# A retention layer and a gated feed-forward on one core: the last 256 tokens of batch 1 in 64-token chunks, with the casts of their states on VectorE, and three state groups of batch 0 as 64x64 tiles

## The chip, the cores and the metric

The kernel runs on one core of a Trainium2 chip. The metric is the device time of one execution in microseconds; the median of three runs of the kernel before is 297.26 us (297.23 to 297.26). A profiled execution of each kernel shows where the time goes: TensorE (PE; PEld are its weight loads), VectorE (DVE), ScalarE (ACT), GpSimd (POOL), and SyncE (SP), which issues nearly all transfers.

## The reference

Eight batches of eight heads, 576 tokens, head size 64. Retention is attention without a softmax: the scores are multiplied by a power of a per-head decay. The result, laid out by token, goes through a feed-forward of width 2048.

```
gamma = 1.0 - 2.0 ** (-5.0 - np.arange(H))
rel = pos[:, None] - pos[None, :]
Dmat = np.where(rel >= 0, gamma[:, None, None] ** rel, 0.0)
attn = np.matmul(scores * Dmat, v)                  # scores = q k^T / 8
x = attn.transpose(0, 2, 1, 3).reshape(B * S, H * D)  # 4608 x 512
h = x @ w_in                                        # 512 x 2048
out = (h / (1 + exp(-beta * h))) @ w_out            # 2048 x 512
```

## The kernel before

Because the decay is a power of the distance, it is split into a factor on q and one on v (`gq`, `gv`), and retention can be done in chunks: inside a chunk the masked scores times v, and from earlier chunks q times a running state, the sum over earlier tokens of k^T v. A state is 64x64 for each head. All matmuls are in bf16 and sum in PSUM, which has eight banks; the tags `mm` (three banks), `O` (two), `sc` (two) and `st` (one) are handed round, and a tile that is written into a bank waits for the reader of the tile before it.

The first 512 tokens of each batch are a block of the feed-forward; the last 64 tokens of all eight batches make a ninth block ("tail"). The feed-forward of a block is a list of fills: `up` (one 128-wide slice of w_in: four matmuls of 512 columns into `mm`, then a ScalarE activation into `gT`; or half a block of tokens, with 256 columns) and `down` (four of the 16 products for 128 tokens; the last four end in a copy and an output transfer). The retention of the next block is put between the fills. `merged` does this by hand-written positions: each step of a stream has a number, and is emitted ahead of the fill of that number. `u1` is the first fill of block 1, `d0` the first `down` of block 0, `base[n]` the first fill of block n. The engines execute in the order of emission, each in its own queue.

Retention is done in three ways.

- Batch 0 works on spans of 256 tokens (`s_T`, `s_sc`, `s_O`, `s_st`, `s_keep`, `s_cross`, `s_x`), at the start of the kernel, when nothing else can fill TensorE. `s_st(a, n, s, rows)` adds k^T v of head group a (four heads) over some rows of a span; with `low` or `high` rows it uses 64 of the 128 rows of the array and all 128 columns. `s_keep` copies the 64x64 blocks on the diagonal into `sbds`, which `s_cross` reads as a 128x128 block-diagonal weight.
- Batch 1 works on chunks of 128 tokens, i = 4 to 7 (`t_k` turns the keys, `a_sc` scores, `a_O` products, `a_cross` states times q, `a_st` states, `a_x` evicts the result). Chunks 4 and 5 come under the last `down` fills of block 0; chunks 6 and 7 under the first `up` fills of block 1. Those first `up` fills go over the first 256 tokens (ten slices in halves) while the last 256 are not there yet.
- Batches 2 to 7 and the tail work on chunks of 64 tokens, with 64x64 tiles in all four quarters of the array (`d_st` states, with a `chain` of sums on VectorE and casts on ScalarE; `d_sc` scores; `d_out` products and crosses). `spread` and `head_of` order the heads so that four matmuls that follow each other use four different quarters. For these, q and k are stored with heads 4 to 7 swapped in pairs (`turned`), from batch `QB` on. In `d_out` a VectorE memset, the fence, separates two sets of matmuls that add to the same PSUM places from different rows of the array.

The keys are cast and the values scaled on GpSimd (`pre`), q of batches 0 and 1 is scaled on VectorE (`pre_q`), and the order of transfers on SyncE is q and kv of batch 1, then of batch 2, and so on.

Of the kernel before, what the change touches and what calls it, by code (L numbers as in the profile page):

```python
# [19 lines left out]
def kernel(  # L20
# [15 lines left out]
    P = 128  # L36
# [33 lines left out]
    QB = 2  # L70
# [211 lines left out]
    def pre_q(b, n):  # L282
# [15 lines left out]
        e.tensor_tensor(batch[b]["qs"][:, cs, hs], q_tiles[b][:, hs, cs].rearrange("p h i d -> p i h d"),  # L298
                        gq[:, cs, hs].unsqueeze(3).to_broadcast([P, cs.stop - cs.start, hs.stop - hs.start, D]),
                        ALU.mult)  # L300
# [97 lines left out]
    def a_cross(i):  # L398

        b, c = seq[i]  # L400
        if c == 0:
            return
        for p in range(HP):
            rhs, view = q_cols(i, slice(0, P), p)
            nc.tensor.matmul(view(O_of(i, p)), sbds[c - 1][:, p, :], rhs, start=False, stop=True, skip_group_check=True)

    def a_O(i):
# [5 lines left out]
        for j, p in [(n % 2, n // 2) for n in range(H)]:  # L413
            nc.tensor.matmul(O_of(i, p)[j * D:(j + 1) * D], vn[:, 2 * p + j, :], R[:, j, p, :],
                             start=opens(i, p), stop=c == 0, skip_group_check=True)
# [11 lines left out]
    def a_st(i):  # L427

        b, c = seq[i]
        if b is None:  # L430
            return
        L = live[i]
        if c == 0:
            state_ps[b] = psum.tile([P, HP, P], F32, name="st", tag="st", bufs=1)
        st = state_ps[b]
        for p in range(HP):
            nc.tensor.matmul(st[:, p, :], heads(L["kn"], p), heads(L["vn"], p),
                             start=(c == 0 and p == 0), stop=True, skip_group_check=True)
        for j in range(2):
            r, cols = slice(j * D, (j + 1) * D), slice(j * D, (j + 1) * D)  # L440
            e = nc.vector.tensor_copy if i in (CB + 2, CB + 3) else nc.scalar.copy
            if c < CB - 1:
                e(sbds[c][r, :, cols], st[r, :, cols])
                continue
            e(ends[b][r, :2], st[r, :2, cols])
            e(ends[b][(1 - j) * D:(2 - j) * D, 2:], st[r, 2:, cols])
# [72 lines left out]
    def s_st(a, n, s, rows, at=None, fresh=False):  # L519
# [4 lines left out]
        S, at = spans[s], 2 * a if at is None else at  # L524
        for i in range(2):
# [31 lines left out]
    def d_sc(u):  # L557

        R = [sb.tile([P, 2, 2, HP, TL], BF16, name="R", tag="R", bufs=4) for _ in range(2)]
        sc = {}  # L560
        for x in range(2):
# [384 lines left out]
```

## Time and profile before

| what | value |
|---|---|
| median of three runs | 297.26 us |
| the profiled execution | 297.28 us |
| its span, first to last instruction | 295.5 us |
| granted TensorE clock | 1.00 throughout |
| VectorE, ScalarE, GpSimd busy | 35%, 49%, 38% |
| transfers, share of 16 engines | over 0.9 for most of the first 220 us |
| all transfers | 53.97 MB in 124033 packets |

The page shows busy time by engine, the span in 40 slices, the chain of work that ended last, and groups of instructions by source line. A matmul's length in the trace runs on past the start of the next one, since matmuls are pipelined; how long one takes in a stream is read from start to start. The field "128*128" of a matmul row is the part of the array, rows by columns, that it uses; "128x512" is what it streams.

Where the changed steps stand, from the timeline (start to start): batch 0's half-row states lie at 12.96, 13.85 and 19.86 us; the retention of batch 1 between 42.1 and 55.4 us; the first `down` of block 1 at 66.2 us; batch 2's retention from 67.2 us on. In the stretch from 43.8 to 55.4 us TensorE is busy all of the time, VectorE 8.0, ScalarE 8.6 and GpSimd 9.2 of its 11.6 us.

### The profile page before, as it was taken

What the parts mean: (1) busy time and instruction counts of PE and PEld (TensorE: products, weight loads), DVE (VectorE), ACT (ScalarE), POOL (GpSimd) and SP (SyncE); (2) the same over time, 40 slices, a digit from 0 to 9 for tenths busy, and PEclk for the clock granted to TensorE, in tenths of its full rate; (3) what the DMA queues carried; (4) which work ended last, traced back from release to release, by engine and by line L of the source; (5) the groups of instructions that cost most, each with busy time, mean ns of one, the idle gap of its engine ahead of it and who ended that gap; (6) DMA issues with size and microseconds to landing.
All of it is one profiled execution on the core that took longest, in us unless ns stands there. A gap on an engine that the chain in (4) does not pass through costs nothing.

```text
span 295.5 us, 7656 instructions
## 1 busy us (share of the span) xinstructions
PE 287.1 (97%) x3245; PEld 150.6 (51%) x3274; DVE 102.5 (35%) x213; ACT 145.9 (49%) x255; POOL 111.1 (38%) x219
## 2 busy tenths in 40 slices
PE   7999999999999999999999999999999999999995
PEld 3654587855544554445444544454554544444443
DVE  5764546604640551045204530354053500110012
ACT  5657537783278434843474347434780167007600
POOL 5957027955733713280438316754223000000000
PEclk9999999999999999999999999999999999999999
DMA  7999999999999898949999849998998110131011
GB/s 225 306 367 386 376 226 277 220 180 253 222 229 235 214 162 231 252 72 161 231 250 198 180 105 273 190 177 180 219 174 138 73 38 0 35 71 38 0 71 71
DMA packets 124033, 53.97 MB, mean 183 GB/s; under 512 B 101840, under 2 KB 116448, under 8 KB 124000
## 3 DMA queue, kind: packets, MB, share of 16 engines
q1 hardware_dynamic: 123968, 53.49, 82.1%
q8 instruction: 25, 0.41, 0.6%
q14 instruction: 8, 0.07, 0.1%
q10 hardware_dynamic: 32, 0.01, 0.0%
HBM read 36.71 MB, written 9.44 MB: 156 GB/s over the span
## 4 chain that ended last, share of the span: by engine, by line
PE 96%; DMA 1%; issue 1%; ACT 0%; DVE 0%; DVEq 0%
PE po L690 42%; PE ph L655 38%; PE ph L670 4%; PE O L614 2%; PE sc L568 1%; PE st L586 1%; DMA qn<-in_q_dram 1%; PE O L627 1%; PE T L352 1%; PE st L527 1%; PE sc L378 0%; PE sc L490 0%; PE O L504 0%; ACT kT L475 0%; PE ph L248 0%
## 5 line engine op out<-in xcount | busy, mean ns | idle before, releaser
L690 PE MATMUL po<-w_out_sb,gT 128*128 128x512 bf16 (+3 forms) x619 | 125.7, 358 | 2.3 <-issue 2.1
L657 ACT ACTIVATE gT<-ph,beta_sb 128x512 bf16<-128x512 f32 (+1 forms) x140 | 91.5, 659 | 50.9 <-PE ph L655 50.5
L655 PE MATMUL ph<-xT,w_in_sb 128*128 128x512 bf16 (+1 forms) x550 | 114.4, 364 | 0.5
L690 PEld LDWEIGHTS <-gT 128*128 128x128 bf16 x636 | 60.2, 98 | 60.7
L655 PEld LDWEIGHTS <-w_in_sb 128*128 128x128 bf16 x560 | 54.3, 98 | 57.5 <-DVE first L594 0.4
L697 DVE COPY ot<-po 128x512 f32<-128x512 f32 (+2 forms) x33 | 22.2, 672 | 72.2 <-PE po L690 69.4
L328 POOL CAST kn<-kvn 128x128 bf16<-128x128 f32 (+2 forms) x76 | 23.4, 343 | 46.1 <-DMA kvn<-in_k_dram 41.2
L295 POOL TENSOR_TENSOR qs<-qn,gq 128x256 bf16<-128x256 f32 (+1 forms) x36 | 26.3, 756 | 33.1 <-DMA qn<-in_q_dram 33.1
L575 DVE TENSOR_TENSOR R<-sc,tri 128x512 bf16<-128x512 f32 x28 | 17.4, 684 | 60.0 <-PE sc L568 60.0
L306 POOL TENSOR_TENSOR vn<-kvn,gv 128x512 bf16<-128x512 f32 x28 | 29.1, 1040 | 7.4 <-DMA kvn<-in_v_dram 7.1
L642 ACT CAST xT<-O 128x512 bf16<-128x512 f32 x14 | 7.5, 590 | 31.6 <-PE O L627 31.6
L597 ACT CAST sbd<-warm 128x256 bf16<-128x256 f32 x18 | 7.3, 407 | 25.6 <-DVE warm L594 20.6
L670 PE MATMUL ph<-xT,w_in_sb 128*128 128x512 bf16 x54 | 12.8, 379 | 0.1
L594 DVE TENSOR_TENSOR first<-st,warm 128x256 f32<-128x256 f32 x24 | 10.2, 425 | 2.9 <-ACT sbq L597 0.5
L316 POOL TENSOR_TENSOR kn<-tln,gq 128x128 bf16<-128x128 f32 (+1 forms) x12 | 5.6, 470 | 14.2 <-DMA tln<-in_q_dram 9.9
L594 DVE TENSOR_TENSOR warm<-st,first 128x256 f32<-128x256 f32 x18 | 7.6, 423 | 9.6 <-PE st L586 8.4
L673 ACT ACTIVATE gT<-ph,beta_sb 128x512 bf16<-128x512 f32 x14 | 8.7, 688 | 4.4 <-PE ph L670 4.4
L642 DVE CAST xT<-O 128x512 bf16<-128x512 f32 x14 | 9.0, 686 | 5.1 <-PE O L627 5.1
L214 POOL CAST w_in_sb<-wt 128x256 bf16<-128x256 f32 (+1 forms) x15 | 7.7, 530 | 5.0 <-DMA wt<-in_moe_w_in_dram 4.9
L597 ACT CAST sbd<-first 128x256 bf16<-128x256 f32 x18 | 7.3, 407 | 2.2 <-DVE first L594 0.2
L670 PEld LDWEIGHTS <-w_in_sb 128*128 128x128 bf16 x56 | 5.2, 97 | 6.3 <-issue 0.5
L231 DVE TENSOR_SCALAR w_out_sb<-wt,rbeta_sb 128x512 bf16<-128x512 f32 x13 | 5.9, 485 | 5.0 <-DMA wt<-in_moe_w_out_dram 5.0
(107 smaller groups left out, 166.1 us busy)
## 6 DMA issues: line engine op xcount, KB each, us to landing
qn<-in_q_dram SPq DMA_DIRECT2D x16, 512.0 KB, 5.2
kvn<-in_k_dram SPq DMA_DIRECT2D x32, 256.0 KB, 6.1
kvn<-in_v_dram SPq DMA_DIRECT2D x32, 256.0 KB, 5.1
out_dram<-ot SPq DMA_DIRECT2D x31, 256.0 KB, 3.4
wt<-in_moe_w_out_dram SPq DMA_DIRECT2D x8, 512.0 KB, 8.5
wt<-in_moe_w_in_dram SPq DMA_DIRECT2D x5, 512.0 KB, 8.8
wt<-in_moe_w_in_dram SPq DMA_DIRECT2D x6, 256.0 KB, 5.6
tln<-in_q_dram SPq DMA_DIRECT2D x8, 128.0 KB, 3.6
```

The source lines that it names most:

```text
L295: nc.gpsimd.tensor_tensor(batch[b]["qs"][:, cs, to], q_tiles[b][:, hs, cs].rearrange("p h i d -> p i h d"), gq[:, cs, hs].unsqueeze(3).to_ ...
L306: nc.gpsimd.tensor_tensor(live[i]["vn"], kv_tiles.pop(i)[:, 1], gains(gv, c), ALU.mult)
L328: nc.gpsimd.tensor_copy(kn[:, c % 2, to], t[:, 0, hs])
L575: nc.vector.tensor_tensor(R[x][:, j].rearrange("k c p q -> k (c p) q"), sc[x, j].rearrange("k c p q -> k (c p) q"), mask, ALU.mult)
L594: nc.vector.tensor_tensor(new[:], add, sums[(c - 1) % 2][:], ALU.add)
L597: nc.scalar.copy((sbq[c] if c < NC - 1 else ends[u])[:], new[:])
L642: (nc.scalar.copy if n % 2 else nc.vector.tensor_copy)(x, o)
L655: nc.tensor.matmul(ph, w_in_sb[:, ko, fo * P:(fo + 1) * P], xts[m][:, ko, :, w], start=(ko == 0), stop=(ko == KO - 1))
L657: nc.scalar.activation(gts[m][:, fo, :, w], ph, ACT.Silu, scale=beta_sb[:, fo:fo + 1])
L670: nc.tensor.matmul(phs[f][:], w_in_sb[:, ko, f * P:(f + 1) * P], xts[m][:, ko], start=(ko == 0), stop=(ko == KO - 1))
L690: nc.tensor.matmul(po[:, x:y], gT[:, fo, ms, :], w_out_sb[:, fo, n0 + x:n0 + y], start=(fo == 0), stop=(fo == FO - 1), skip_group_check=m ...
L697: (nc.scalar.copy if m == 0 else nc.vector.tensor_copy)(ot, po[:, :nn])
```

## The change

Batch 1's chunks 6 and 7 (256 tokens) leave the 128-token way. They become four chunks of 64 tokens, by `late_scores` (at u1 + 3: `d_st(1, 1)`, then `d_sc` of the second half alone, then the `chain`, with its casts on VectorE, then the two masks) and a new `half_out` (at u1 + 12), which is `d_out` for half a batch. The first 256 tokens stay in two chunks of 128, but states are now kept as 64x64 tiles in `sbq` and as fp32 sums in `sums`, so that the chain can go on from them: `a_st` uses 128x64 tiles, `a_cross` 64x64 tiles, and `a_keep` copies. For that batch 1 takes the swapped order of heads (QB = 1): heads 4 to 7 of its q are scaled in two steps each, and its keys are cast in three steps each on GpSimd. `t_k(7)` moves ahead of the first `up` fill of block 1.

The number of `up` slices of block 1 in halves goes from 10 to 15 (NH). Products of `down` that are split into two of 256 columns: block 0 from slice 8 on (before: from 5), block 1 from slice 12 on (before: none). In batch 0, `s_st` of heads 0 to 3 over half the rows uses 64x64 tiles, two for each pair of heads, and the first such group comes ahead of the whole-span group.

```diff
-    QB = 2
+    QB = 1
...
         if b < 2:
             hs, cs = slice(n // 2 * HP, (n // 2 + 1) * HP), slice(n % 2 * 2, n % 2 * 2 + 2)
-            e = nc.vector
+            for to, hs in [(hs, hs)] if n < 2 or b < QB else turned[1:]:
+                nc.vector.tensor_tensor(batch[b]["qs"][:, cs, to], ..., ALU.mult)
...
     def a_cross(i):
         b, c = seq[i]
-        if c == 0:
-            return
         for p in range(HP):
-            rhs, view = q_cols(i, slice(0, P), p)
-            nc.tensor.matmul(view(O_of(i, p)), sbds[c - 1][:, p, :], rhs, start=False, stop=True, skip_group_check=True)
+            for j in range(2):
+                rhs, view = q_cols(i, half(j), p)
+                nc.tensor.matmul(view(O_of(i, p)[half(head_of(b, p, j) % 2)]), sbq[2 * c - 1][half(j), p, :], rhs,
+                                 start=False, stop=True, skip_group_check=True)
...
     def a_st(i):
...
+        for p in range(HP):
+            for j in range(2):
+                nc.tensor.matmul(state_ps[b][half(j), p, :], L["kn"][:, 2 * p + j, :], L["vn"][:, head_of(b, p, j), :],
+                                 start=c == 0 and p == 0, stop=True, skip_group_check=True)
+
+    def a_keep(i):
+        b, c = seq[i]
+        nc.scalar.copy(sbq[2 * c + 1][:], state_ps[b][:])
+        if c:
+            nc.vector.tensor_copy(sums[c % 2][:], state_ps[b][:])
...
     def s_st(a, n, s, rows, at=None, fresh=False):
...
+        if a == 0 and rows != whole_span:
+            for i in range(2):
+                for p in range(2):
+                    for j in range(2):
+                        nc.tensor.matmul(s_sts[n][half(j), at + p, half(j)], S["kn"][rows, i, 2 * p + j, :],
+                                         S["vn"][rows, i, 2 * p + j, :], start=fresh and i == 0 and p == 0, stop=True,
+                                         skip_group_check=True)
+            return
...
-        def chain():
-            for c in range(4 * x, 4 * x + 4):
-                new, add = sums[c % 2], S[c % 2][:, c // 2 % 2]
+        def chain(cs=range(4 * x, 4 * x + 4), e=nc.scalar.copy):
+            for c in cs:
+                new, add = sums[c % 2] if u != 1 or c < NC - 1 else ends[u], S[c % 2][:, c // 2 % 2]
...
-                nc.scalar.copy((sbq[c] if c < NC - 1 else ends[u])[:], new[:])
+                if new is not ends[u]:
+                    e((sbq[c] if c < NC - 1 else ends[u])[:], new[:])
...
+    def half_out(u):
+        O = {(hh, y): psum.tile([P, 2, CB, 2, TL // CB], F32, name="O", tag="sc" if y else "O", bufs=2)
+             for y in range(2) for hh in range(2)}
...
+        for other in range(2):
+            for n in range(16):
+                cl, pp, y, hh = n // 8, n // 4 % 2, n // 2 % 2, n % 2
+                p, j = pp + 2 * y, hh if other else 1 - hh
...
+                last = nc.tensor.matmul(to(CB + 2 * cl + hh, p, h % 2), piece(u, CB + 2 * cl)["vn"][half(hh), h, :],
+                                        columns(u, batch[u]["R"][1][half(hh), j, cl, p, :]), ...)
+            if not other:
+                fence = nc.vector.memset(fenced[:], 0.0)
+                after(fence, last)
+        for flip in range(2):
+            for n in range(16):
...
+                m = nc.tensor.matmul(to(c, p, j ^ y), sbq[c - 1][half(j), p, :], q_of(u, c, j, p),
+                                     start=False, stop=True, skip_group_check=True)
+                if flip and n < 2:
+                    after(m, fence)
+        for n, ((hh, y), o) in enumerate(O.items()):
+            x = xt(u)[:, 2 * y:2 * y + 2, :, MB // CB // 2:].rearrange("k p i (c h s) -> k (p i) c h s", c=2, h=2)
+            (dve, act)[n % 2](x[:, :, :, hh, :], o.rearrange("k p i c s -> k (p i) c s"))
...
-            parts = ((0, nn),) if m or fo < 5 else ((0, nn // 2), (nn // 2, nn))
+            parts = ((0, nn),) if m > 1 or fo < (12 if m else 8) else ((0, nn // 2), (nn // 2, nn))
...
+    s_st(0, 0, 0, low)
     s_st(0, 1, 0, whole_span)
+    s_keep(0, 0, (act, act))
     s_keep(0, 1, (act, act))
-    s_st(0, 0, 0, low)
-    s_keep(0, 0, (act, act))
...
-    u1 = len(fill)
-    fill += [F(up, 1, fo, 2 * x, 2) for x in range(2) for fo in range(10)]
-    fill += [F(up, 1, fo) for fo in range(10, FO)]
+    u1, NH = len(fill), 15
+    fill += [F(up, 1, fo, 2 * x, 2) for x in range(2) for fo in range(NH)]
+    fill += [F(up, 1, fo) for fo in range(NH, FO)]
...
     def second(i):
-        for f in (a_O, a_cross, a_x):
-            f(i)
-            f(i + 1)
-        a_st(i + 1)
+        a_O(i)
+        a_O(i + 1)
+        a_st(i + 1)
+        a_cross(i + 1)
+        a_x(i)
+        a_x(i + 1)
+        a_keep(i + 1)
+
+    def late_scores():
+        chain, masks = d_st(1, 1), d_sc(1, (1,))
+        chain((4, 5, 6, 7), dve)
+        masks(1)
...
-                (d0 + 15.95, F(t_k, 6)), (u1 + 1, F(t_k, 7)), (u1 + 2, F(a_sc, 6)), (u1 + 3, F(a_sc, 7)),
-                (u1 + 4, F(a_st, 6)), (u1 + 7, F(second, 6))]]
+                (d0 + 15.95, F(t_k, 6)), (d0 + 15.96, F(t_k, 7)), (u1 + 3, late_scores), (u1 + 12, F(half_out, 1))]]
```

TensorE's program grows from 6542 to 6798 rows of matmuls and weight loads; the rows of SyncE are the same in number and order.

More of the change, by code (lines that the diff above doesn't have):

```diff
@@ L413, in a_O @@
         for j, p in [(n % 2, n // 2) for n in range(H)]:
-            nc.tensor.matmul(O_of(i, p)[j * D:(j + 1) * D], vn[:, 2 * p + j, :], R[:, j, p, :],
+            h = head_of(b, p, j)
+            nc.tensor.matmul(O_of(i, p)[half(h % 2)], vn[:, h, :], R[:, j, p, :],
                              start=opens(i, p), stop=c == 0, skip_group_check=True)
@@ L429, in a_st @@
         b, c = seq[i]
-        if b is None:
-            return
         L = live[i]
         if c == 0:
-            state_ps[b] = psum.tile([P, HP, P], F32, name="st", tag="st", bufs=1)
-        st = state_ps[b]
+            state_ps[b] = psum.tile([P, HP, D], F32, name="st", tag="st", bufs=1)
         for p in range(HP):
[L437 to L446, printed above, removed]
+            for j in range(2):
[6 more added lines that the diff above has]
+            nc.vector.tensor_copy(sums[c % 2][:], state_ps[b][:])
     spread = [(0, 0), (1, 1), (0, 1), (1, 0)]
@@ L579, in d_st @@
     def d_st(u, x):
[L581 removed]
+        S = [psum.tile([P, 2, HP, D], F32, name="st", tag=t, bufs=n) for t, n in (("st", 1), ("O", 2) if u == 1 else ("mm", 3))]
         for cl in range(2):
```

30 lines of the change are left out of this document (18 added, 12 removed).

## The prediction

> **What bounds the kernel now.** I read the page first, then the chain of waits, then the timelines of TensorE, ScalarE and VectorE around the places that the change touches. The page's busy times, slices and chain:
>
> ```profile
> PE 287.1 (97%) x3245; PEld 150.6 (51%) x3274; DVE 102.5 (35%) x213; ACT 145.9 (49%) x255; POOL 111.1 (38%) x219
> ...
> PE   7999999999999999999999999999999999999995
> ...
> PE 96%; DMA 1%; issue 1%; ACT 0%; DVE 0%; DVEq 0%
> ```
>
> TensorE is busy in every slice and is 96% of the chain; the list of TensorE's own waits holds 4.4 us in all, 1.8 of it for VectorE in the first 6 us and 2.1 without any releaser. So an edit is worth what it takes from TensorE's instruction stream, unless a wait takes its place. The stretch that is rewritten, on TensorE's timeline (start, length; the length runs past the next start, so I use start to start):
>
> ```profile
> 46.57 0.40 PE L378 MATMUL sc<-qT,kT 64*128 64x128 bf16 x8
> 46.90 0.40 PE L437 MATMUL st<-vn,kn 128*128 128x128 bf16 x4
> 47.13 1.04 PE L690 MATMUL po<-w_out_sb,gT 128*128 128x256 bf16 x8
> 48.10 0.66 PE L414 MATMUL O<-R,vn 128*64 128x128 bf16 x16
> ...
> 49.50 0.61 PE L655 MATMUL ph<-xT,w_in_sb 128*128 128x256 bf16 x4
> 49.94 0.39 PE L358 MATMUL T<-ident,kn 128*128 128x128 bf16 x4
> 50.17 0.60 PE L655 MATMUL ph<-xT,w_in_sb 128*128 128x256 bf16 x4
> 50.70 0.53 PE L378 MATMUL sc<-qT,kT 64*128 64x128 bf16 x8
> 51.16 0.61 PE L655 MATMUL ph<-xT,w_in_sb 128*128 128x256 bf16 x4
> ...
> 54.10 0.64 PE L414 MATMUL O<-R,vn 128*64 128x128 bf16 x16
> 54.67 0.62 PE L405 MATMUL O<-qT,sbd 128*128 128x128 bf16 x8
> 55.13 0.39 PE L437 MATMUL st<-vn,kn 128*128 128x128 bf16 x4
> 55.35 0.82 PE L655 MATMUL ph<-xT,w_in_sb 128*128 128x256 bf16 x6
> ```
>
> Four whole-array matmuls of 128 columns take 0.22 us (55.13 to 55.35), 56 ns each. Where the shape in the array changes (the field 128*128, 64*128, 64*64) the single records behind these lines stand 146 to 151 ns apart in place of 56: about 0.1 us for each change. What 64x64 pieces cost, later in the same kernel:
>
> ```profile
> 71.97 0.45 PE L586 MATMUL st<-vn,kn 64*64 64x64 bf16 x32
> 72.24 0.76 PE L568 MATMUL sc<-qT,kT 64*64 64x64 bf16 x64
> 73.15 5.99 PE L690 MATMUL po<-w_out_sb,gT 128*128 128x512 bf16 x27 [0.16 <-issue]
> ```
>
> 32 of them take 0.27 us, 8.5 ns each, since four run side by side (records 3, 4, 3 and 22 ns apart).
>
> **The change, part by part.**
>
> *Batch 1's second half.* Removed: from 49.50 to 55.35 TensorE spends 5.85 us; in it are 7 half blocks of fill (28 matmuls of 256 columns at 109.2 ns, 3.06) and one transpose group (0.23) that stay. So 2.56 us go: two score groups, two state groups, 16 products, 8 cross products, and three changes of shape each way. Added: late_scores, 32 state and 32 score matmuls: entry 0.09, 0.27, 0.29 (half of the 0.57 that L568's 64 take), and 0.13 to get out less 0.03 of the last four = 0.75. half_out, 64 matmuls: the same entry and exit, and 0.55 for 64 (L614, 79.07 to 79.62) = 0.77. Its fence: in the last batch's products the records stop 0.13 us at the fence of L618 with 32 matmuls between, as here; I take 0.12. Together 1.64 us, so -0.92 before waits.
>
> *The wait for VectorE.* half_out needs both masked scores and all four PSUM banks, which VectorE gives back. Its work after the state matmuls is now one chain: 4 sums, 3 casts (they were ScalarE's), 2 masks. The rows:
>
> ```profile
> 67.67 0.42 DVE L596 COPY warm<-st 128x256 f32<-128x256 f32 x1 [10.17 <-issue]
> 68.20 0.42 DVE L594 TENSOR_TENSOR first<-st,warm 128x256 f32<-128x256 f32 x1
> ```
>
> ```profile
> 19.18 0.42 DVE L216 CAST w_in_sb<-wt 128x256 bf16<-128x256 f32 x2
> 20.77 0.70 DVE L216 CAST w_in_sb<-wt 128x256 bf16<-128x256 f32 x2 [1.16 <-DMA wt<-in_moe_w_in_dram]
> ```
>
> The chain starts 0.50 us after the first state matmul (67.17 to 67.67). A step that needs the one before takes 0.53 start to start; a cast of 128x256 lasts 0.22 to 0.49, and I take 0.35 to the next start, nearer the slow ones since GpSimd is busy from 50.74 on here as it was at 20.77. Then 3 x 0.53 + 3 x 0.35 + 0.36 + masks 0.61 + 0.69 (L575: 0.684) = 4.30, so the masks end 4.80 and are seen 0.06 later, 4.86 us after that matmul. TensorE comes after 0.27 + 0.26 + 0.13 + 9 half blocks (3.93) + 0.09 = 4.68. Wait 0.18 us; from 0 (casts at 0.22) to 1.07 (casts 0.49, every step dependent). What is queued behind it on TensorE is everything; behind the casts on VectorE are only the masks and half_out's own evictions.
>
> The Trainium skill, "TensorEngine Tiling", section "PSUM Bottleneck", speaks against this change: tiling makes TensorE faster but not the reading of PSUM, which may become the limit. The rows agree that VectorE's 4.3 us stand against TensorE's 0.5 here; by the rule alone, with no cover, the sum would lose the gain, and with the nine half blocks as cover it is the 0.18 above.
>
> *Batch 1's first half.* The state group in 128*64 shape costs about what it did: entry and exit instead of one exit; +0.02. Then products, states and crosses in three shapes, and both transposes directly behind. The second transpose writes the PSUM bank that ScalarE's last eviction frees:
>
> ```profile
> 48.21 0.59 ACT L697 COPY ot<-po 128x512 f32<-128x512 f32 x1
> 48.69 0.59 ACT L425 CAST xT<-O 128x512 bf16<-128x512 f32 x1
> 49.17 0.39 ACT L423 CAST xT<-O 128x256 bf16<-128x256 f32 x1
> ```
>
> That row ends 1.46 us after 48.10; with 0.05 to be seen and 0.22 for the transpose the first half block starts 1.73 us after L414's start, against 1.40 + 0.23 = 1.63 before: +0.11 (0 if ScalarE is quicker, 0.2 if the crosses are slower). The 64-column products in pairs (128*64) have no row: 32 ns a pair by the quads, 56 by L414's pairs, which is 0.1 us more in each of two groups; I take the quads.
>
> *Batch 0.* Three half-row state groups go to 64*64, and two of the three then stand beside groups of that shape: three changes of shape less. But ScalarE sets the next step there: six casts (L536, from 13.06, 1.76 us) end at 14.82, and the cross product that needs the last starts at 14.87. They can begin once ScalarE's copy at 12.38 is done (12.97), so 0.1 us comes through (0 to 0.15) of the 0.4 that TensorE saves. The third group (19.86) keeps both its changes: -0.05 (0 to -0.09).
>
> *Fill.* Splitting a 512-column matmul costs 2 x 109.2 - 215.8 = 2.6 ns. 12 fewer in batch 0, 16 and 20 more in batch 1: +0.06.
>
> *Costed at nothing.* GpSimd's key casts become three each: 0.87 in place of 0.61 (L328: 79.93 starts, three in 0.87). They sit in its waits for DMA (0.77, 0.59 and 0.61 us idle at 43.49, 46.87, 48.10), so values 6 and 7 still end at 50.22, and the state matmuls come at 51.1; without that cover it would be 4 x 0.26. The q product of batch 1 in four pieces ends near 41.7 against a use at 43.4. half_out's evictions take 0.8 us on two engines under three half blocks (1.31). ScalarE's 30 half activations come every 0.437, TensorE's own pace, and two in a row stood 0.39 apart. No DMA is added or moved in any queue.
>
> Sum: -0.92 + 0.18 + 0.02 + 0.11 - 0.10 - 0.05 + 0.06 = -0.70 us. The profiled execution took 297.28 with a span of 295.5; 294.8 then, and on the median of 297.26, 296.55 us.
>
> **Rivals.**
> 1. *The chain on VectorE decides.* Casts at 0.49 and all steps dependent: wait 1.07, so 296.55 + 0.89 = 297.4; halfway 297.0. For it: the slow casts are those beside GpSimd. Against: at 19.18 two took 0.42. No change.
> 2. *The gain is handed back to a transfer.* The last tail's transpose is issued at 223.15, and landings take 3.1 to 5.7 us, so 226.3 to 228.9; it is read about 0.3 us after 227.92. If loads came no earlier, some 0.5 us of lead would be left: 296.8. Against: these loads queue behind output copies that wait for TensorE, so they move too. Batch 2's last key transpose (issued 65.19, so by 70.9, read from 72.24) has room.
> 3. *Slower: instruction supply.* TensorE's stream grows by 256 rows, and twice (80.10 and 213.74) a 64*64 group stops some 0.09 us at a matmul that waits for nothing, each near a 16 KB instruction fetch (81.25, 214.11). If each of the some 16 groups of that shape caught such a stop, +1.4: 297.95. It decides from 14 groups on; before it was two.
> 4. *64 columns as dear as 128.* 16 quads' matmuls of 128 columns take 0.25 us (13.28 to 13.53), 15.6 ns each; 128 x 7.1 ns = 0.9: 297.45. The rows of 32 in 0.27 speak against it. The skill's "TensorEngine Tiling", section "Instruction Overhead", says the like: some 60 cycles of overhead on every matmul, so that narrow ones gain nothing. The rows of 64*64 groups do not show it.
>
> **How the numbers follow.** Forecast 0.53; rival 1 0.20; rival 2 0.08; rival 3 0.13 (with any other loss of its size); rival 4 0.03; small gains lost elsewhere 0.03. A measurement here can tell about 0.2% (0.6 us) from no change, so faster means below 296.67: the forecast alone, though its own range, 296.2 to 296.9, crosses that; a part of it goes to "same" and a part of rival 1 (no wait at all) comes back. Faster 0.53, same 0.34, slower 0.13. The range, 296.15 to 297.4, takes in rivals 1 and 2.
>
> **What would show it.** The group of 64 matmuls of half_out starting 4.7 to 4.9 us after late_scores' first; a VectorE row of four sums and three casts before it in 3.0 us; the second transpose starting at ScalarE's 49.5; 64*64 rows of 32 in 0.27; the fence stop of about 0.1. It is wrong if TensorE stands over 0.4 us before half_out, or if a later batch's groups wait for a transpose.

## The result, and the profile after

The changed kernel takes 296.52 us (median of 16 runs, 295.71 to 297.08) beside 296.8 us of the kernel before on the same chip (16 runs). The ratio is 0.9982 with a 95% interval of [0.9974, 0.9990]: 0.53 us faster, 0.3 to 0.77. The prediction was 0.70 us faster. The profiled executions are further apart, 297.28 and 296.29 us (spans 295.5 and 294.5); why is part of what follows.

The page of the changed kernel: busy time by engine, TensorE's slices, the chain that ended last.

```profile
PE 288.4 (98%) x3402; PEld 151.9 (52%) x3402; DVE 101.6 (34%) x216; ACT 146.1 (50%) x260; POOL 112.7 (38%) x227
...
PE   7899999999999999999999999999999999999995
...
PE 95%; DMA 1%; ACT 1%; DVE 1%; issue 0%; DVEq 0%
```

TensorE bounds it as before. The rewritten stretch on TensorE's timeline (start, length, line, group):

```profile
48.16 0.64 PE L413 MATMUL O<-R,vn 128*64 128x128 bf16 x16
48.63 0.29 PE L434 MATMUL st<-vn,kn 128*64 128x64 bf16 x8
48.85 0.31 PE L402 MATMUL O<-qT,sbd 64*64 64x128 bf16 x8
49.10 0.40 PE L356 MATMUL T<-ident,kn 128*128 128x128 bf16 x4
49.68 0.38 PE L356 MATMUL T<-ident,kn 128*128 128x128 bf16 x4 [0.18 <-ACT xT L422]
49.90 1.47 PE L694 MATMUL ph<-xT,w_in_sb 128*128 128x256 bf16 x12
51.30 0.45 PE L590 MATMUL st<-vn,kn 64*64 64x64 bf16 x32
51.58 0.46 PE L572 MATMUL sc<-qT,kT 64*64 64x64 bf16 x32
51.97 4.10 PE L694 MATMUL ph<-xT,w_in_sb 128*128 128x256 bf16 x36
56.00 0.45 PE L665 MATMUL O<-R,vn 64*64 64x64 bf16 x32
56.28 0.26 PE L676 MATMUL O<-qT,sbd 64*64 64x64 bf16 x10
...
56.77 2.47 PE L694 MATMUL ph<-xT,w_in_sb 128*128 128x256 bf16 x21
```

The products, states and crosses of batch 1's first half come in three shapes (48.16 to 49.10). The late scores take 0.67 us (51.30 to 51.97), half_out 0.77 (56.00 to 56.77). The group at 56.00 carries no wait: it starts 4.70 us after the states at 51.30, when TensorE gets there. The second transpose waits 0.18 us for ScalarE's eviction, so the first half block starts 1.74 us after 48.16. VectorE's chain under it:

```profile
51.80 0.42 DVE L598 TENSOR_TENSOR warm<-st,first 128x256 f32<-128x256 f32 x1 [0.78 <-PE st L590]
52.26 0.29 DVE L602 CAST sbd<-warm 128x256 bf16<-128x256 f32 x1
52.47 0.42 DVE L598 TENSOR_TENSOR first<-st,warm 128x256 f32<-128x256 f32 x1
...
53.79 0.42 DVE L598 TENSOR_TENSOR end<-st,warm 128x256 bf16<-128x256 f32 x1
54.13 1.28 DVE L579 TENSOR_TENSOR R<-sc,tri 128x512 bf16<-128x512 f32 x2
```

It ends at 55.41, 4.11 us after the first state matmul; the casts took 0.29 us each. At the start there are two new gaps, first on TensorE and then the ScalarE copies that make the first of them:

```profile
13.82 0.25 PE L525 MATMUL st<-vn,kn 64*64 64x64 bf16 x4 [0.29 <-ACT sbd L540]
...
17.75 0.38 PE L709 MATMUL ph<-xT,w_in_sb 128*128 128x512 bf16 x1
18.40 1.69 PE L709 MATMUL ph<-xT,w_in_sb 128*128 128x512 bf16 x7 [0.27 <-issue]
```

```profile
12.68 1.09 ACT L540 CAST sbd<-st 64x128 bf16<-64x128 f32 x4
14.18 0.53 ACT L540 CAST sbd<-st 64x128 bf16<-64x128 f32 x2 [0.41 <-PE st L525]
```

The low rows of the second span add into the bank that the whole-span copy, now second in ScalarE's queue, must read first. The gap after 17.75 waits for nothing that the profile shows ("issue").

Where the time went, start to start on TensorE's timelines, for all kernels that were run. The first column begins at the third score group of batch 0, 12.28 us before and 12.09 in the changed kernel:

| kernel | third score group to first out product | to batch 2's first 64x64 states | to the last out product |
|---|---|---|---|
| before | 19.37 | 35.53 | 224.98 |
| changed | 19.62 | 34.75 | 224.69 |
| e1_batch1_only | 19.48 | 35.16 | 226.83 |
| e1b_rows_back | 19.80 | 34.75 | 225.17 |
| e2_batch0_only | 19.56 | 35.52 | 225.03 |
| e3_old_order | 19.76 | 34.95 | 225.17 |
| e4_less_cover | 19.46 | 36.32 | 224.96 |
| e5_turn_later | 19.73 | 34.97 | 225.35 |
| e6_shift16 | 21.13 | 34.75 | 225.18 |
| e7_before_shift16 | 19.75 | 35.52 | 224.78 |
| e8_no_split | 19.38 | 34.68 | 231.44 |
| e9_casts_act | 19.71 | 35.61 | 225.28 |
| e10_keys_first | 19.95 | 34.75 | 224.94 |
| e11_batch1_keys_first | 19.37 | 34.75 | 224.98 |

In the two profiles: 0.25 lost with batch 0, 0.78 won with batch 1, 0.29 won later, where the change touches nothing, and 0.19 ahead of that score group (12.28 against 12.09), where it touches nothing either. Together 1.01, of the 0.99 between the profiled times. The last two vary from execution to execution: the first transpose of q, which waits for a transfer and VectorE, starts at 5.79 us before and 5.69 after, and at 5.46 to 6.07 in the other profiles; and the last column is 224.94 to 225.28 in the other runs with batch 1's change, where no long wait or stop falls into it.

### The profile page after: what moved, and what is told of

Its sections match the earlier page's. It is cut to its first block, busy times and chain, and to the rows that moved or that the text cites. A ratio compares the mean times of both kernels' runs of the same rounds, so it can differ in the third digit from the quotient of the medians.

```text
span 294.5 us, 7957 instructions
## 1 busy us (share of the span) xinstructions
PE 288.4 (98%) x3402; PEld 151.9 (52%) x3402; DVE 101.6 (34%) x216; ACT 146.1 (50%) x260; POOL 112.7 (38%) x227
## 4 chain that ended last, share of the span: by engine, by line
PE 95%; DMA 1%; ACT 1%; DVE 1%; issue 0%; DVEq 0%
PE po L729 43%; PE ph L694 38%; PE ph L709 4%; PE st L590 2%; PE O L619 2%; PE sc L572 2%; DMA qn<-in_q_dram 1%; PE O L632 1%; PE T L350 1%; PE st L531 0%; DVE R L489 0%; ACT kT L471 0%; ACT sbd L540 0%; PE sc L486 0%; PE ph L248 0%
## 5 line engine op out<-in xcount | busy, mean ns | idle before, releaser
L729 PE MATMUL po<-w_out_sb,gT 128*128 128x512 bf16 (+3 forms) x640 | 128.9, 358 | 0.0
L694 PEld LDWEIGHTS <-w_in_sb 128*128 128x128 bf16 x580 | 56.4, 98 | 55.2 <-DVE first L598 0.5
L326 POOL CAST kn<-kvn 128x128 bf16<-128x128 f32 (+1 forms) x84 | 24.6, 332 | 45.1 <-DMA kvn<-in_k_dram 45.1
L579 DVE TENSOR_TENSOR R<-sc,tri 128x512 bf16<-128x512 f32 x30 | 18.6, 682 | 59.9 <-PE sc L572 59.9
L598 DVE TENSOR_TENSOR warm<-st,first 128x256 f32<-128x256 f32 x20 | 8.4, 422 | 10.4 <-PE st L590 9.2
L709 PEld LDWEIGHTS <-w_in_sb 128*128 128x128 bf16 x56 | 5.3, 98 | 6.5 <-issue 0.6
```

The costliest lines, as they stand in the source:

```text
L326: nc.gpsimd.tensor_copy(kn[:, c % 2, to], t[:, 0, hs])
L579: nc.vector.tensor_tensor(R[x][:, j].rearrange("k c p q -> k (c p) q"), sc[x, j].rearrange("k c p q -> k (c p) q"), mask, ALU.mult)
L598: nc.vector.tensor_tensor(new[:], add, sums[(c - 1) % 2][:], ALU.add)
L694: nc.tensor.matmul(ph, w_in_sb[:, ko, fo * P:(fo + 1) * P], xts[m][:, ko, :, w], start=(ko == 0), stop=(ko == KO - 1))
L709: nc.tensor.matmul(phs[f][:], w_in_sb[:, ko, f * P:(f + 1) * P], xts[m][:, ko], start=(ko == 0), stop=(ko == KO - 1))
L729: nc.tensor.matmul(po[:, x:y], gT[:, fo, ms, :], w_out_sb[:, fo, n0 + x:n0 + y], start=(fo == 0), stop=(fo == FO - 1), skip_group_check=m < 2)
```

## The experiments

Each set has its own runs of the kernel before, whose medians were 297.39, 297.12 and 297.5 us; so kernels are compared by their ratios to it. The three sets hold e1 to e4, then e1b, e9, e5, e8, then the last four.

**e1_batch1_only and e2_batch0_only: the two parts alone.** Batch 0's groups and order are undone in the first, and are all that is changed in the second.

```diff
-        if a == 0 and rows != whole_span:
-            ... (64x64 tiles)
-    s_st(0, 0, 0, low)
     s_st(0, 1, 0, whole_span)
-    s_keep(0, 0, (act, act))
     s_keep(0, 1, (act, act))
+    s_st(0, 0, 0, low)
+    s_keep(0, 0, (act, act))
```

> The change's batch 1 part alone: the four half-row state groups of batch 0 are again 128x128 matmuls in the old order; all splits of fill stay. Theory (the gain is made in batch 1's second half, between 51 and 58 us, and batch 0's part is worth nothing: 0.08 us lost at the start by a wait for ScalarE's copies, 0.08 won in the late products): the stretch from the first scores (L486) to batch 0's first products, 4.46 us in the changed kernel, is 4.38 again, with no wait of TensorE for the s_keep copies; the time is the changed kernel's within 0.15 us, 0.4 to 0.7 us under the kernel before. Rival A (batch 0's part makes the gain): no faster than before, 0.4 to 0.6 us over the changed kernel. Rival B (the stops in the instruction stream decide): the new stop of some 0.3 us at 17.75 us goes with the changed row count, and the time falls a further 0.2 to 0.3 us.

> The kernel before with the change's batch 0 part alone: three half-row state groups as 64x64 matmuls, and the new order of the first groups and copies. Theory: same as before within 0.15 us: start 0.08 us later for the wait on ScalarE, late products 0.08 us earlier. Rival A (batch 0's part makes the gain): 0.3 to 0.6 us faster. Rival B (instruction supply): a stop of 0.2 to 0.4 us at about 17.75 us as in the changed kernel, since the rows up to there are the same but for the splits, so 0.1 to 0.3 us slower than before; or the stops that the kernel before has at 80 and 214 us move.

Measured: batch 1 alone 1.0001 [0.9983, 1.0020], batch 0 alone 1.0004 [0.9993, 1.0015]. Batch 0's part is worth nothing, as the theory had it: it loses 0.19 us by the table. But the theory missed batch 1 alone: its stretch is 0.37 us shorter than before and nothing is left of it. The time alone would fit rival A; e2_batch0_only speaks against it, and e11 below does too. The twelve executions spread from 295.63 to 298.31 us, and the profiled one took 298.18, so its waits are not those of every execution. TensorE's timeline of e1_batch1_only at batch 2's scores and at the last ones:

```profile
71.34 0.44 PE L564 MATMUL sc<-qT,kT 64*64 64x64 bf16 x32
72.59 0.45 PE L564 MATMUL sc<-qT,kT 64*64 64x64 bf16 x32 [0.82 <-DMA kT<-kn]
```

```profile
227.82 0.58 PE L564 MATMUL sc<-kT 64*64 64x64 bf16 x48
229.28 0.32 PE L564 MATMUL sc<-kT 64*64 64x64 bf16 x16 [0.89 <-DMA kT<-kn]
```

Both waits are for transposed keys: the gain is handed to transfers, rival 2 of the prediction. Why the keys were late is shown only in part. A load is reported in 16 parts; of some loads, the issue time and the landing of the parts (us), with the start of the 16 KB instruction fetch ahead of them:

```
kernel           fetch   load, issued   15th part   16th part
e1_batch1_only   41.85   v    36.59       42.84       44.37
                         v    39.59       43.79       45.30
changed          40.02   v    36.60       42.89       43.28
                         v    39.59       43.84       44.27
changed          57.06   k    54.26       58.59       60.13
                         v    55.27       59.69       61.04
```

One part is 1.4 to 1.5 us behind the other 15 in three of these cases, with a fetch while the loads are under way; at the fetch of 40.02 it is 0.4. In e1_batch1_only the later loads are then issued later than in the changed kernel (45.11 against 43.97, 50.62 against 49.42), and so is batch 2's second key transpose (67.14 against 65.95, landed 72.55 against 70.77). The kernel before has two fetches between 40 and 62 us (40.21, 52.73), the changed one three (40.02, 52.21, 57.06), since it runs more rows there. Batch 2's second key transpose landed at 69.60 before and at 70.77 after. It is read by the second 32 of the score matmuls, from 72.50 and 71.81 on: 2.9 us of lead before, 1.0 after. (The expectations below count to the first score matmul and have 2.6 and 0.7.)

**e1b_rows_back: the same with 24 rows of idle work.** Twelve products that feed nothing put the rest of TensorE's stream back where it lies in the changed kernel.

```diff
     betas_safe()
+    for _ in range(12):
+        nc.tensor.matmul(idle_ps[:, :2], sbds[0][:, 0, :], sbds[0][:, 0, :2], start=True, stop=True, skip_group_check=True)
```

> The batch 1 part alone (as e1_batch1_only) with 12 idle products added early, while TensorE waits for the first q transfer: they feed nothing and put TensorE's later instructions at the same place in its stream as in the changed kernel (24 rows more). In e1_batch1_only the instruction fetch of the stretch came at 41.85 us instead of 40.0, one of a load's 16 parts then landed 1.5 us after the other 15 (44.37 against 42.84), and TensorE later waited 1.0 us for batch 2's keys and 1.1 us for the last batch's. Theory (where the fetches fall in the loads decides e1_batch1_only's loss, not batch 0's part): the fetch comes at 39.5 to 40.5 us again, the load lands by 43.5, the two waits for kT shrink to under 0.3 us together, and the time falls by 1.0 us or more, to the changed kernel's within 0.3 us. Rival A (batch 0's part itself is what keeps the keys in time): fetch or no fetch, the waits for kT stay over 0.5 us each and the time stays within 0.3 us of e1_batch1_only's. Rival B (chance of a single execution): the fetch moves but the median stays.

Measured: 0.9982 [0.9970, 0.9995]. The fetch came at 40.14, the load landed at 43.20, the first wait shrank to 0.21 us and the second is gone. So the waits went as the theory had it, but its chain is not shown: the transpose was issued at 67.75, later than in e1_batch1_only, and landed at 71.97, still 1.2 us after the changed kernel's. The place of the fetch is a part of the lateness at most, and each kernel has one profile. The time is weak too: the ratio fell by 0.0019 (0.56 us, not the 1.0 expected), and its interval overlaps that of e1_batch1_only.

**e3_old_order: the 64x64 tiles, with the whole-span group first again.**

```diff
-    s_st(0, 0, 0, low)
     s_st(0, 1, 0, whole_span)
-    s_keep(0, 0, (act, act))
     s_keep(0, 1, (act, act))
+    s_st(0, 0, 0, low)
+    s_keep(0, 0, (act, act))
```

> The changed kernel with the 64x64 groups kept, but with the first group of the whole span and its copies ahead of the low half's group again. Theory (the new order puts the copy that TensorE needs second on ScalarE, which costs the 0.25 us wait at 13.82): the wait at L525 for ScalarE goes, the start's stretch (L486 to the first products of batch 0, 4.46 us) becomes 4.2 to 4.35 us, and the time falls by 0.1 to 0.25 us. Rival A (ScalarE sets the stretch whatever the order, as the prediction had it): another wait for ScalarE of the same size takes its place, 4.4 to 4.5 us, no change. Rival B (instruction supply): the stretch changes as in either case, but the stop at 17.75 us grows or shrinks by as much, since it ends with a fetch and not with an instruction.

Measured: 0.9974 [0.9959, 0.9988], not told apart from the changed kernel. The wait at L525 went, but the cross products now wait 0.16 us for ScalarE, and the "issue" gap grew from 0.27 to 0.46 us at the same matmul. It ended 2.45 us after a fetch had begun, in the changed kernel 2.67 us after: rival B. What was saved ahead of it was given back here.

**e4_less_cover: three half blocks less between the late scores and half_out.**

```diff
-                ... (u1 + 3, late_scores), (u1 + 12, F(half_out, 1))]]
+                ... (u1 + 3, late_scores), (u1 + 9, F(half_out, 1))]]
```

> The changed kernel with the out group of batch 1's last tokens called three half blocks of fill earlier (6 in place of 9 between the scores and it). Theory (VectorE's chain of 4 sums, 3 casts and 2 masks ends 4.11 us after the first state matmul and TensorE reaches the group at 4.70, so 0.53 us of cover are to spare): TensorE would come 1.31 us earlier, at 3.39, so a wait of 0.75 to 0.85 us for VectorE appears at the group (L653 on), the time rises by 0.7 to 0.85 us, and the three half blocks moved behind it change nothing. Rival A (the group doesn't need the end of the chain: it starts on sums that are done earlier): no wait, no change. Rival B (GpSimd's casts or another engine slow the chain at its old place): the chain ends at another time than 4.1 us and the wait is under 0.5 or over 1.0 us.

Measured: 1.0025 [1.0010, 1.0039], 1.3 us over the changed kernel by the ratios; the wait is twice what was expected, as large as rival B had it. VectorE, then TensorE:

```profile
52.51 0.71 DVE L602 CAST sbd<-warm 128x256 bf16<-128x256 f32 x1
...
53.59 0.29 DVE L602 CAST sbd<-first 128x256 bf16<-128x256 f32 x1
...
54.25 0.68 DVE L602 CAST sbq<-warm 128x256 bf16<-128x256 f32 x1
...
55.19 1.27 DVE L579 TENSOR_TENSOR R<-sc,tri 128x512 bf16<-128x512 f32 x2
```

```profile
51.55 0.45 PE L590 MATMUL st<-vn,kn 64*64 64x64 bf16 x32
...
56.51 0.44 PE L665 MATMUL O<-R,vn 64*64 64x64 bf16 x32 [1.50 <-DVE R L579]
```

So the group does need the end of the chain, and the chain was 4.91 us long here, not 4.11: two of three casts took 0.7 us in place of 0.29 while GpSimd scaled batch 2's q (from 52.46 on). The Trainium skill, "SBUF — State Buffer", section "Who interferes with whom", has a rule for it: a VectorE cast and a GpSimd instruction can want the same pair of ports, and the later one stands still until the earlier is done. The rows agree: the two slow casts began inside a GpSimd instruction (52.51 in one from 52.46 to 53.07, 54.25 in one from 53.66 to 54.78) and ended 0.15 us after it. In the changed kernel GpSimd was as busy, from 52.26 on, but each cast began with one of its instructions or in the last 0.11 us of one. In the ten profiled executions with the chain on VectorE it ends 4.10 to 5.07 us after the first state matmul (changed kernel 4.11, e11 4.42, e10 4.62, e1b 4.63, e3 4.85, e1 5.07). The changed kernel's profile is one of the two luckiest (the other is e8's, 4.10).

**e9_casts_act: the three casts on ScalarE.**

```diff
-        chain((4, 5, 6, 7), dve)
+        chain((4, 5, 6, 7), act)
```

> The changed kernel with the three casts of the late chain on ScalarE, between its silu halves, in place of VectorE. In the changed kernel's profile each cast took 0.29 us on VectorE and the chain ended 0.53 us before TensorE needed it; in the profiles of e3_old_order, e4_less_cover and e1_batch1_only two of the three took 0.64 to 0.76 us beside GpSimd, the chain ended 4.85 to 5.07 us after the first state matmul, and TensorE waited 0.15 to 0.3 us where it comes after 4.70. Theory (that contention costs about 0.2 us in most executions, not in the one profiled): VectorE's chain ends 3.4 to 3.8 us after the first state matmul, no wait at the out group, 0.1 to 0.3 us faster than the changed kernel unless ScalarE's silu halves fall behind. Rival A (the chain has cover in most executions): no change within 0.1 us. Rival B (ScalarE is as tight: its silu halves come at TensorE's own pace of 0.437 us, so three casts of some 0.38 put it 1.1 us behind, and TensorE waits for a PSUM bank of the fill): 0.3 to 0.8 us slower, with waits of TensorE for ScalarE's gT between 52 and 57 us.

Measured: 1.0004 [0.9989, 1.0019], 0.65 us over the changed kernel, at the edge of what the two intervals tell apart. The profile is that of rival B, though from the slowest of the twelve executions: VectorE's chain was 3.64 us long, but TensorE's fill stood:

```profile
52.42 1.48 PE L694 MATMUL ph<-xT,w_in_sb 128*128 128x256 bf16 x12
54.60 2.78 PE L694 MATMUL ph<-xT,w_in_sb 128*128 128x256 bf16 x24 [0.69 <-ACT gT L696]
```

**e5_turn_later: the second key transpose one fill later.**

```diff
-                (d0 + 15.96, F(t_k, 7)), ...
+                (u1 + 1, F(t_k, 7)), ...
```

> The changed kernel with the second key transpose of batch 1's last tokens one fill item later again (a half block between the two transposes), as it was in the kernel before. Theory (the prediction's +0.11: the second transpose waits 0.18 us for ScalarE's last eviction): the wait at L356 goes, the first half block starts 0.18 us earlier, and 0.1 to 0.2 us are won, if VectorE's copy of the keys (0.37 us) still comes before its sums. Rival A: the delay of the transpose delays the late scores' keys, and the same 0.2 us is lost again there as a wait of L572 for kT. Rival B (transfers, not TensorE, end last): TensorE is 0.15 us earlier until 66 us and the gain is gone at batch 2's keys (landed 70.77, first read about 71.5 in the changed kernel).

Measured: 0.9981 [0.9967, 0.9995], no change, and none of the three had it right. The wait stays where it is and has another waiter, the half block now in front, which reads the same evicted columns:

```profile
49.22 0.61 PE L694 MATMUL ph<-xT,w_in_sb 128*128 128x256 bf16 x4 [0.18 <-ACT xT L422]
```

Batch 2's keys landed late as well in this execution (a wait of 0.46 us).

**e8_no_split: all out products of the fill whole.**

```diff
-            parts = ((0, nn),) if m > 1 or fo < (12 if m else 8) else ((0, nn // 2), (nn // 2, nn))
+            parts = ((0, nn),)
```

> The changed kernel with no split in any out product of the fill (the 48 matmuls of 512 columns that it does in two halves are whole again): 96 rows fewer in TensorE's stream, 64 of them before 50 us. Theory A (the splits only cost 2.6 ns each): 0.12 us less on TensorE by batch 2's states, and no new stop. Theory B (the splits let GpSimd, ScalarE or the loads slip in, or keep the instruction supply fed): a wait of over 0.2 us appears in batch 0's or batch 1's out products. Beside these: the instruction fetch of 57.06 us, which holds one part of three loads back by 1.5 us, moves to 59 to 62 us; batch 2's last key transpose then lands earlier than 70.77 us if that fetch was what made it late, and the same if the loads are held by something else.

Measured: 1.0251 [1.0221, 1.0281], 7 us slower, foreseen by neither theory in size or place. Up to batch 2's states it is 0.07 us quicker, as splits at 2.6 ns each would make it. The loss is later, in code that is the same; TensorE's timeline, and then its busy time, granted clock (third column from the end), transfer share and GB/s in the stretch behind:

```profile
167.44 0.19 PE L632 MATMUL O<-qT,sbd 64*64 64x64 bf16 x1
170.84 0.21 PE L632 MATMUL O<-qT,sbq 64*64 64x64 bf16 x1 [3.20 <-issue]
```

```profile
172.90:174.50 1.60, 1.60 (x6) 0.50 (x5) 0.73 (x2) 1.02 (x3) 0.00 (x0) 0.50 0.00 0
```

A stop of 3.4 us inside a group of 64x64 matmuls, then 512 columns in 427 ns in place of 216 until the clock is back (1.7 us lost), and a second stop of 0.93 us at 205.40. Both end 2.44 and 2.55 us after an instruction fetch began (168.40, 202.85). With 96 rows fewer, the stream seems to run dry at other places; that is how I read it, and all six executions were slow (303.11 to 305.81). The fetch expected at 59 to 62 us came at 58.51, and batch 2's last keys landed at 71.09, no earlier than before.

**e6_shift16 and e7_before_shift16: 16 idle products (32 rows) early,** as in e1b_rows_back, in the changed kernel and in the kernel before.

> The changed kernel with 16 idle products (32 rows of TensorE's stream) added early, while TensorE waits for the first q transfer; they feed nothing. Theory (instruction supply: stops and fetches stand at places in the stream, not at places in the work): the stop at 17.75 us, 0.43 us beyond a matmul's time in the changed kernel and 0.27 to 0.63 in three others with the same rows before it, changes by over 0.2 us or goes, and the fetches come 1 to 3 us earlier than 40.0 and 57.06 us; the time moves by 0.2 to 1.0 us, in either direction. Rival (the stop belongs to the work there, a wait that the profile doesn't show): the stop stays 0.25 to 0.65 us at the same matmul, the time within 0.15 us of the changed kernel's.

> The kernel before with the same 16 idle products early. Its computation and its order are those of the kernel before. Theory (places of the fetches move the time by some tenths in any kernel of this length, and a part of the change's 0.5 us may be such luck): the stops of 0.09 to 0.10 us at 80.10, 83.87 and 213.74 us move or go, others may come, and the time differs from the kernel before by 0.2 to 0.8 us, in either direction. Rival (the kernel before, with 2.6 us of lead for its keys, doesn't care where the fetches fall): the same stops within 0.05 us and the time within 0.15 us.

Measured: 1.0025 [1.0006, 1.0043] and 1.0020 [0.9999, 1.0041]. In the changed kernel the stop left its matmul and stands in the group before it, 1.74 us beyond a matmul's time in place of 0.43:

```profile
16.72 0.58 PE L500 MATMUL O<-R,vn 64*64 64x128 bf16 x27
18.84 0.30 PE L500 MATMUL O<-R,vn 64*64 64x128 bf16 x5 [1.54 <-issue]
```

It ends 2.56 us after the fetch of 16.28. Counted in rows it has not moved: in both kernels it stands after 223 weight loads and 223 matmuls of TensorE's stream. The starts of the matmuls on both sides of that row, in six profiles (us):

| kernel | fetch | 223rd matmul | 224th matmul | from fetch to 224th |
|---|---|---|---|---|
| before | 16.12 | 19.93 | 19.98 | 3.86 |
| e11_batch1_keys_first | 16.24 | 20.14 | 20.20 | 3.96 |
| e8_no_split | 16.14 | 18.15 | 18.55 | 2.41 |
| changed | 15.73 | 17.75 | 18.40 | 2.67 |
| e3_old_order | 15.60 | 17.20 | 18.05 | 2.45 |
| e6_shift16 | 16.28 | 17.08 | 18.84 | 2.56 |

Of the other eight, e1_batch1_only comes to the row 3.99 us after the fetch and does not stop; the other seven start the 224th 2.4 to 2.6 us after. So TensorE gets past this row no sooner than 2.4 us after the fetch, and stands for what is missing. The stop belongs to a place in the stream, not to the work there. Narrow groups add rows ahead of it and so bring TensorE there earlier; the idle rows of e1b and e7, whose groups are 128 wide, do the same. The time of e6 moved more than expected, by 1.3 us, and its later fetches (39.57, 58.65) did not come 1 to 3 us earlier.

In the kernel before the stops at 80.10, 83.87 and 213.74 went, as expected, and were worth 0.2 us (224.78 against 224.98). Its start lost 0.38 us: 0.07 at the same row, and 0.31 in a wait for values that GpSimd scales, where GpSimd's first key cast began at 8.33 us in place of 7.38:

```profile
13.20 0.71 PE L527 MATMUL st<-vn,kn 128*128 128x128 bf16 x8 [0.25 <-POOL vn L467]
```

Whether the time moved is not settled by that interval.

**e10_keys_first and e11_batch1_keys_first: batch 2's second key transpose ahead of two loads,** in the changed kernel and in e1_batch1_only.

```diff
-                st += [(at - 30.1, F(load_kv, n)), (at - 30, F(x_k, XB, 1)), (at - 30, F(load_kv, n + 1))]
+                st += [(at - 30.2, F(x_k, XB, 1)), (at - 30.1, F(load_kv, n)), (at - 30, F(load_kv, n + 1))]
```

> The changed kernel with batch 2's second key transpose queued ahead of the two loads of batch 3 that stand before it in SP's queue (the only edit; TensorE's stream is the same row for row). In the changed kernel it lands at 70.77 us and is first read at about 71.5, so 0.7 us of lead are left, where the kernel before had 2.6 (69.60 against 72.24). Theory (in part of the executions this lead is used up, and the gain goes to a wait for keys, as in the profiles of e5_turn_later with 0.5 us and e1_batch1_only with 0.9): the transpose lands 1.0 to 1.5 us earlier, no wait for kT at batch 2, and the median falls by 0.1 to 0.3 us below the changed kernel's. Rival A (the lead is enough in nearly all executions): same within 0.1 us. Rival B (the two loads, now behind the transpose, come late for batch 3's keys, or the last batch's transposes do): a wait for kT at 79 to 106 us or at 227, and 0.2 to 1.0 us slower.

> The same move of batch 2's second key transpose ahead of two loads, in e1_batch1_only, where TensorE waited 0.9 us for these keys and 0.8 us for the last batch's. Theory (the delayed loads, by whatever fetch, only matter through the lead of the two transposes): the wait at 71.6 us shrinks from 1.0 to under 0.2 us and the time falls by 0.5 to 1.0 us, the wait at 228 staying about as it was. Rival A (all of the queue is late, so moving one transpose only moves the wait to the loads behind it): the wait goes elsewhere and the median stays within 0.2 us of e1_batch1_only's. Rival B (the wait at 228 grows by what is won at 71.6, since the last transposes land by the clock and not behind TensorE): TensorE is 0.9 us earlier until 227 and the time is the same.

Measured: 0.9978 [0.9961, 0.9996] and 0.9969 [0.9951, 0.9987]. In e10 the keys landed at 67.6, 5 us ahead; the time is not told apart from the changed kernel's (rival A, or less of a gain than these runs can show). In e11 they landed at 69.85 in place of 72.55, and batch 2's scores run through:

```profile
71.75 0.75 PE L564 MATMUL sc<-qT,kT 64*64 64x64 bf16 x64
```

The wait at 228 went too, which neither theory had; the ratio fell by 0.0032, some 0.95 us, as the theory had it. The fetch was still at 41.73, and the second load of v still had one part 0.94 us late. So the lag is harmless where the lead is large. e11 keeps only batch 1's part and has the lowest ratio of all, but its interval overlaps the changed kernel's: it is not shown to be faster.

## Why the prediction was right, step by step

- **Batch 1's second half: right.** The steps in that stretch without the wait were -0.92, +0.02, +0.11 and eight splits more (+0.02), -0.77; the table shows -0.78 in every execution with no wait (-0.85 in e8, without its splits). The parts agree: late_scores 0.67 plus the entry (0.76 against 0.75), half_out 0.77 plus the entry (0.86 against 0.77 and 0.12 for the fence, whose stop is 0.125), the first half block 1.74 us after the products (1.73).
- **The wait for VectorE: right in kind, and a matter of chance.** Forecast 4.86 us of chain and 0.18 of wait. The profile after shows 4.11 and none, which alone would call the step wrong; over ten executions the chain is 4.10 to 5.07. Nine of the ten have the nine half blocks as cover: three lose 0.20 (e3), 0.22 (e5) and 0.41 us (e1) there by the table, six nothing, so 0.09 us in the mean.
- **Batch 0: wrong in sign.** Forecast -0.10 for the first two narrow groups and -0.05 for the third. The 64x64 kernels need 19.38 to 19.95 us for that stretch (mean of eight without idle rows 19.65), the 128-wide ones 19.37 to 19.48 (mean 19.41): +0.24. It has three parts. From the third score group to the second cross products (17.42 us in the changed kernel) it is +0.06: there the step that failed is that of the six casts on ScalarE. I moved them earlier as a block and did not ask which of them the next state group must wait for, once the copy of the whole span stands second. From there to the third state group (20.01) it is +0.26, the stop at 17.75, which the sum had at nothing and rival 3 at 0.09. The third group is worth -0.08, as forecast. So most of the loss is the stop, which the rows of the narrow groups bring about.
- **Rival 3, instruction supply: not what decided, but real, and larger than priced.** I gave each stop 0.09 us. The larger ones are 0.27 to 3.4 us, and 32 or 96 rows decide where they fall. The changed kernel pays 0.27 us at 17.75, and in its profile the small stops of the kernel before are gone (-0.29 us after 67 us). The second is luck: e10, with the same stream of TensorE row for row, has 0.11 us of such a stop at 79.96, and 224.94 us in the table against 224.69. The 2.1 us without a releaser that the prediction listed are another thing, matmuls missing from the trace: from the states at 67.17 to the next matmul recorded, at 67.77, it is 0.23 us longer than in the changed kernel (66.47 to 66.84), about one matmul of 512 columns, while both take 4.80 us to the next states (71.97, 71.27).
- **Rival 2, transfers: real.** It did not show in the profile after. It shows in e1_batch1_only and e5_turn_later, with waits of 0.46 to 0.9 us. The prediction looked for it at the end of the kernel and said that batch 2's keys had room; their lead was the one that shrank most, from 2.9 to 1.0 us. At the end there was little before and after: the last keys landed 0.22 us ahead of their reading (228.10, 228.32) and 0.13 us (227.20, 227.33).
- **The sum.** -0.78 for batch 1, +0.24 for batch 0, and +0.09 for the wait are -0.45, inside the measured 0.3 to 0.77. The prediction's -0.70 came from the same first term, with a batch 0 that it took 0.4 us too well and a wait 0.1 us too long. What remains of the difference is as large as what the position of the stops does by chance. That the forecast of 296.55 us lies next to the 296.52 measured is luck: it was counted from 297.26, the median of three executions of the kernel before, and sixteen give 296.80.

## What to carry to other kernels

A rewrite into narrow matmuls is priced by TensorE's start-to-start times, and these held here, to 0.01 us in the sum of the stretch; but it also moves every later instruction in the stream, and a few dozen rows moved the time by more than the change itself (1.3 us in e6). So before a change of 0.2% is believed, run it with a few idle rows added, and its parts alone. A chain that one profile shows with cover to spare is read in several executions, above all where GpSimd is busy beside VectorE. And a lead of transfers is compared before and after: the engine that comes earlier takes it from one side, the loads from the other.

## What was not expected of the hardware

- A stop of TensorE with no releaser ends 2.4 to 2.7 us after a 16 KB instruction fetch begins: 15.73 to 18.40 (changed), 15.60 to 18.05 (e3), 16.28 to 18.84 (e6), 168.40 to 170.84 and 202.85 to 205.40 (e8). The first stands at the same row of the stream in eleven profiles. The Trainium skill, "Runtime: NRT & Kernel Launch", section "Instruction fetch mechanics", describes a FIFO that is refilled in blocks of 16 KB and calls the fetch mostly hidden; the blocks agree, the hiding does not hold at these places, which stand in or behind groups of 64x64 tiles. Why the fetch of 168.40 began only a microsecond after the stop stays open.
- A fetch shows in transfers too: one of the 16 parts of the loads under way lands 0.4 to 1.9 us after the others (the 1.9 in e1b: 58.92 and 60.79), where loads that land between fetches have 0.1 to 0.2 (47.77 and 48.69 us in the changed kernel). The two come together in time; that the one causes the other is not tested.
- After a stop of 3.4 us the granted clock was 0.50 for 3.4 us (171.35 to 174.76, e8); after one of 1.74 us there was no such stretch (e6). In e6, e8, e10 and e11 it was 0.50 for 3.4 us near the start too, from 7.5 us on (8.3 in e10).
